# A fused attention, FFN and channel-mix kernel: first products of zeros, first values of v on GpSimd, u turned later, the last sum sorted by halves

## The chip, the core and the metric

The kernel runs on one core of a Trainium2 chip. The metric is the device time of one execution in microseconds (us). The engines are TensorE (PE in the profile, its weight loads PEld), VectorE (DVE), ScalarE (ACT), GpSimd (POOL) and SyncE (SP), which here only issues DMAs; rows named SPq and ACTq are DMAs issued by SyncE and ScalarE.

## The reference

Three layers follow each other on 4 sequences of 3072 tokens with 256 features. All is float32.

```python
scores = (1 / S) * np.matmul(z, z.transpose(0, 2, 1))     # z: 4 x 3072 x 64
attn = np.maximum(scores, 0.0) ** 2
x = u * np.matmul(attn, v)                                # u, v: 4 x 3072 x 256
h = x @ w_in                                              # 256 -> 2048
x = (h - np.tanh(h)) @ w_out                              # 2048 -> 256
x_prev = x shifted by one token within its sequence
xk = mu_k * x + (1.0 - mu_k) * x_prev
xr = mu_r * x + (1.0 - mu_r) * x_prev
k = np.maximum(xk @ w_k, 0.0)                             # 256 -> 1024
out = 1.0 / (1.0 + np.exp(-(xr @ w_r))) * (k * k @ w_v)   # 1024 -> 256
```

## The kernel before

Features lie on the partitions and tokens on the free axis. The 12288 tokens are cut into 24 tiles of 512, six to a sequence. Every float32 operand is split into a high part that TensorE's fast float32 form holds exactly and the low rest (in the code `h` and `l`), and a product is made in three passes: high by high, high by low, low by high (`PASSES`). For the scores the two parts of z lie on the two halves of the partitions, so two passes do.

The work is a list of units. For attention, unit (A, t, p) makes the scores of 256 keys by the 512 queries of tile t (4 products into a buffer `w_A`), applies relu and square on ScalarE, splits the result into h and l, and two units later (`LAG = 2`) multiplies it with v into the sum `acc_A` of its tile: 12 products, two groups of 128 keys by two halves of 128 features by three passes. Scores are symmetric: in the first tile of a sequence, units 2 to 11 also turn their block on VectorE (`keep`, tile `k`) and store it, so that later tiles load it instead of making it. After the 24 x 12 attention units come the units of the FFN (H, 8 to a tile) and of the channel mix (K, 4 to a tile, and R, one).

`produce(n)` writes unit n, `consume(n - 2)` writes the products of two units before; each engine executes its instructions in the order in which they were written. Small side work stands in a list of tasks, each with a first and a last unit between which `run_steps` puts it, within an estimated budget of VectorE time per unit. Loads are bound to a unit by `load(n, ...)`; nearly all are issued by SyncE in order.

What the change touches:

- The start (line 670 on): z groups 0 and 1 are loaded, turned on VectorE (L109), rounded (L110) and split (L87). A group of v (512 keys) is loaded as `vr`, rounded to its high part on ScalarE (L84) and its low part subtracted on VectorE (L87) in `v_steps`. Group 0 is done ahead of the first unit, groups 1 to 5 of the first sequence are tasks.
- `omu`, one minus the mixing vectors, and a `zero` column are made on VectorE at unit 1 (L693, L694).
- u of tile t is loaded in 8 pieces (`u_load`, L158), turned on VectorE (`u_turn`, L167), and multiplied with the finished sum (L487).
- The end: `out_steps` multiplies the K sum with the sigmoid (L539), turns it (L549) and stores it in 8 pieces (L554), half of the features at a time. The last tile's out_steps is the end of the kernel.

The names in the rows: `w_A` the scores, `a_A` the squared scores, `h_A` and `l_A` their parts, `acc_A` and `acc_K` the sums, `zt` and `z` the turned and the split z, `sg` the sigmoid, `o` and `ot` the result before and after its turn.

## Time and profile before

| | us |
|---|---|
| median of 3 runs (2593.69 to 2595.20) | 2593.92 |
| the profiled execution | 2593.08 |
| its span from first to last instruction | 2591.3 |
| TensorE busy, 11328 products | 2572.6 (99%) |
| VectorE busy | 1656.8 (64%) |
| ScalarE busy | 1417.3 (55%) |
| GpSimd busy, 4 instructions | 0.2 |

An engine's busy share is a mean over the whole run: VectorE's 64% is made of stretches near 100% in the first 60 us and of some 55% from the FFN on. An idle stretch matters where TensorE, which is busy 99%, waits for it. Products overlap: the duration of one (0.39 us at full pace) is longer than the distance to the next, which is what counts.

### The profile page before, as it was taken

Reading aid. Unit: us, or ns where it says so; the run is one execution under the profiler, and the core shown is the slowest. Engines: PE = TensorE matmul, PEld = TensorE weight load, DVE = VectorE, ACT = ScalarE, POOL = GpSimd, SP = SyncE. Lnnn points to the kernel's source line nnn. Section 1 sums busy time; section 2 is a strip of 40 time slices with the busy share of each in tenths; the row PEclk is TensorE's granted clock in tenths of the full one; section 3 lists DMA queues with packets and bytes.
Section 4 is the critical chain, followed back from the end, with each engine's and each line's share of the span. In section 5 each row is a group of like instructions: output and inputs, shape, how many; then the busy total and the mean of one; then the engine's idle time right before and its main releaser. Section 6 shows DMA issues by size and latency. Waiting matters only on the chain.

```text
span 2591.3 us, 28822 instructions
## 1 busy us (share of the span) xinstructions
PE 2572.6 (99%) x11328; PEld 2127.7 (82%) x11328; DVE 1656.8 (64%) x1966; ACT 1417.3 (55%) x1632; POOL 0.2 (0%) x4
## 2 busy tenths in 40 slices
PE   8999999999999999999999999999999999999998
PEld 6888888888888888888888888888888888888887
DVE  8788878887798666555555555555555555555554
ACT  7766876776587654444444444444444444444443
POOL 0000000000000000000000000000000000000000
PEclk9999999999999999999999999999999999999999
DMA  8698579668957850000000000000000000000000
GB/s 208 202 230 220 182 213 250 194 189 229 244 183 211 220 174 9 17 17 17 17 17 10 12 17 13 17 17 17 17 17 17 17 17 17 17 17 17 17 9 17
DMA packets 370680, 229.18 MB, mean 88 GB/s; under 512 B 262640, under 2 KB 336368, under 8 KB 370544
## 3 DMA queue, kind: packets, MB, share of 16 engines
q1 hardware_dynamic: 369488, 227.22, 33.3%
q8 instruction: 88, 1.44, 0.2%
q14 instruction: 48, 0.39, 0.1%
q10 hardware_dynamic: 1056, 0.13, 0.0%
HBM read 126.62 MB, written 94.63 MB: 85 GB/s over the span
## 4 chain that ended last, share of the span: by engine, by line
PE 98%; DVE 1%; ACT 0%; SPq 0%; issue 0%; DMA 0%; DVEq 0%
PE acc_A L476 29%; PE acc_H L476 20%; PE w_H L417 20%; PE acc_K L476 10%; PE w_K L417 10%; PE w_A L397 3%; PE w_A L396 3%; PE w_R L441 3%; DVE v L87 0%; SPq L99 0%; DMA vr<-in_v_dram 0%; ACT v L84 0%; ACT a_A L318 0%; SPq L158 0%; DVE k L341 0%
## 5 line engine op out<-in xcount | busy, mean ns | idle before, releaser
L476 PE MATMUL acc_H<-h_H,w_out 128*128 128x512 f32 x1536 | 504.4, 389 | 0.0
L417 PE MATMUL w_H<-xh,w_in 128*128 128x512 f32 x1536 | 500.9, 389 | 0.0
L476 PE MATMUL acc_A<-h_A,v 128*128 128x512 f32 x1344 | 441.0, 390 | 2.2 <-DVE v L87 1.8
L84 ACT ACTIVATE h_H<-g_H 128x1024 fp32r<-128x1024 f32 x192 | 203.6, 1061 | 387.0 <-DVE g_H L431 387.0
L87 DVE TENSOR_TENSOR l_H<-g_H,h_H 128x1024 fp32r<-128x1024 f32 x192 | 235.3, 1225 | 216.5 <-ACT h_H L84 216.5
L431 DVE TENSOR_TENSOR g_H<-w_H,g_H 128x1024 f32<-128x1024 f32 x192 | 233.7, 1217 | 169.4 <-ACT g_H L430 169.4
L476 PEld LDWEIGHTS acc_H<-h_H,w_out 128*128 128x128 f32 x1536 | 288.5, 188 | 59.7
L417 PEld LDWEIGHTS w_H<-xh,w_in 128*128 128x128 f32 x1536 | 288.5, 188 | 59.6
L430 ACT ACTIVATE g_H<-w_H 128x1024 f32<-128x1024 f32 x192 | 195.8, 1020 | 241.7 <-PE w_H L417 241.4
L476 PE MATMUL acc_A<-h_t,v 128*128 128x512 f32 x960 | 310.1, 389 | 0.0
L417 PE MATMUL w_H<-x,w_in 128*128 128x512 f32 x768 | 299.2, 390 | 0.0
L476 PE MATMUL acc_H<-l_H,w_out 128*128 128x512 f32 x768 | 299.1, 389 | 0.0
L476 PEld LDWEIGHTS acc_A<-h_A,v 128*128 128x128 f32 x1344 | 252.2, 188 | 56.2 <-DVE v L87 3.0
L318 ACT ACTIVATE a_A<-w_A 128x1024 f32<-128x1024 f32 (+1 forms) x169 | 172.7, 1022 | 194.1 <-PE w_A L397 193.9
L476 PE MATMUL acc_A<-l_A,v 128*128 128x512 f32 x672 | 262.2, 390 | 1.5 <-DVE l_A L87 1.0
L476 PE MATMUL acc_K<-h_K,w_v 128*128 128x512 f32 x768 | 252.1, 389 | 0.0
L417 PE MATMUL w_K<-mkh,w_k 128*128 128x512 f32 x768 | 252.0, 389 | 0.0
L87 DVE TENSOR_TENSOR l_A<-a_A,h_A 128x1024 fp32r<-128x1024 f32 (+1 forms) x169 | 201.4, 1192 | 56.5 <-ACT h_A L84 55.7
L476 PEld LDWEIGHTS acc_A<-h_t,v 128*128 128x128 f32 x960 | 180.3, 188 | 37.3
L341 DVE STREAM_TRANSPOSE k<-a_A 128x512 f32<-128x512 f32 x240 | 156.2, 689 | 83.7 <-ACT a_A L319 83.3
L322 DVE CAST h_K<-a_K 128x1024 fp32r<-128x1024 f32 x96 | 66.7, 695 | 212.8 <-ACT a_K L319 212.8
L476 PE MATMUL acc_A<-l_t,v 128*128 128x512 f32 x480 | 186.9, 389 | 0.0
(122 smaller groups left out, 3500.3 us busy)
## 6 DMA issues: line engine op xcount, KB each, us to landing
at<-k SPq DMA_DIRECT2D x120, 512.0 KB, 3.3
b<-at SPq DMA_DIRECT2D x240, 256.0 KB, 5.9
vr<-in_v_dram SPq DMA_DIRECT2D x24, 512.0 KB, 6.9
uin<-in_u_dram SPq DMA_DIRECT2D x192, 64.0 KB, 2.9
x1d<-x SPq DMA_DIRECT2D x24, 512.0 KB, 3.1
x<-x1d SPq DMA_DIRECT2D x24, 512.0 KB, 3.8
out_dram<-ot SPq DMA_DIRECT2D x192, 64.0 KB, 1.9
zin<-in_z_dram SPq DMA_DIRECT2D x94, 64.0 KB, 4.5
```

The costliest lines, as they stand in the source:

```text
L84: nc.scalar.activation(out=o, in_=i, func=ACTF.Copy)
L87: nc.vector.tensor_tensor(out=o, in0=i, in1=hi.bitcast(F32), op=ALU.subtract)
L318: nc.scalar.activation(out=a[:, x], in_=w[:, x], func=ACTF.Relu, scale=sc)
L322: high(h[:, x], a[:, x])
L341: nc.vector.transpose(out=t[:, :, :, c].rearrange("p b a j -> p a b j"), in_=a[:, c].rearrange("p (a b i) -> p a b i", a=4, b=4),)
L396: nc.tensor.matmul(w[:, j], lhsT, z1[b, g], start=True, stop=False)
L397: nc.tensor.matmul(w[:, j], lhsT, z2[t], start=False, stop=True)
L417: nc.tensor.matmul(w[:, j], ws[wt, f // 4][a][:, c, (f % 4) * P : (f % 4 + 1) * P], x[m][:, c], start=n == 0, stop=n == 3 * DC - 1,)
L430: nc.scalar.activation(out=g, in_=w, func=ACTF.Tanh)
L431: nc.vector.tensor_tensor(out=g, in0=w, in1=g, op=ALU.subtract)
L441: nc.tensor.matmul(w[:, d], ws["r", 0][a][:, c, d * P : (d + 1) * P], x[m][:, c], start=n == 0, stop=n == 3 * DC - 1,)
L476: nc.tensor.matmul(o[:, c], w[a][:, c * P : (c + 1) * P], s[m][:, j], start=p == 0 and j == 0 and n == 0, stop=p == last and j == 1 and n ...
```

## The change

Five things change.

- Ahead of the first scores, GpSimd clears a tile of zeros and TensorE makes 11 products of it into a score buffer that nobody reads.
- For the first sequence, groups 1 to 5 of v are rounded and subtracted on GpSimd instead of ScalarE and VectorE; their tasks cost nothing in the budget, their deadlines and the raw loads of groups 3 to 5 are a little earlier. Group 0 stays where it was, but is written behind the first unit instead of ahead of it. `zero` and `omu` go to GpSimd too.
- u of tile t is loaded one unit into its tile (the first at unit 5) and turned from its tile's sixth unit on; before, it was loaded a tile earlier.
- In the last K unit the 12 products are sorted by half of the features, and the last K sum lies in two buffers of one half each.
- The last tile's end works on quarters: half of the features by half of the tokens, with the four stores of each quarter alternating between SyncE's and ScalarE's queue.

```diff
--- before.py
+++ after.py
@@ -139,14 +139,21 @@
 
         def high():
             st["w"] = w = big(f"v{b}_{g}").rearrange("p (l c d) -> p l c d", l=2, c=4)
-            copy_hi(w[:, 0], vraw[b, g])
+            if b or not g:
+                copy_hi(w[:, 0], vraw[b, g])
+            else:
+                nc.gpsimd.tensor_copy(w[:, 0], vraw[b, g])
 
         def low():
             w = st["w"]
-            sub_lo(w[:, 1], vraw.pop((b, g)), w[:, 0])
+            x = vraw.pop((b, g))
+            if b or not g:
+                sub_lo(w[:, 1], x, w[:, 0])
+            else:
+                nc.gpsimd.tensor_tensor(out=w[:, 1], in0=x, in1=w[:, 0].bitcast(F32), op=ALU.subtract)
             vs[b, g] = w
 
-        return [(0.0, high), (1.3, low)]
+        return [(0.0, high), (1.3 if b else 0.0, low)]
 
     def u_load(t):
         a = p4(f"uin{t}", shape=(P, DC, 16, 32))
@@ -451,9 +458,14 @@
             split[unit] = s
 
     def get_acc(kind, t):
+        if (kind, t) not in acc and kind == "K" and t == NT - 1:
+            acc[kind, t] = [
+                ps.tile([P, 512], F32, tag="acc", name=f"acc_{kind}{t}_{c}", bufs=2) for c in range(DC)
+            ]
         if (kind, t) not in acc:
             acc[kind, t] = ps.tile([P, 2, 512], F32, tag="acc", name=f"acc_{kind}{t}", bufs=2)
-        return acc[kind, t]
+        a = acc[kind, t]
+        return a if isinstance(a, list) else [a[:, c] for c in range(DC)]
 
     def consume(unit):
         kind, t, p = unit
@@ -462,24 +474,27 @@
         s = split.pop(unit)
         o = get_acc(kind, t)
         last = {"A": NP, "H": NH, "K": NK}[kind] - 1
+        w = []
         for j in range(2):
             f = 2 * p + j
             if kind == "A":
                 kp = pairs[t % NG][p]
                 f = kp // 2 * 4 + kp % 2 + 2 * j
-            if kind == "A":
-                w = [vs[t // NG, f // 4][:, l, f % 4] for l in range(2)]
+                w.append([vs[t // NG, f // 4][:, l, f % 4] for l in range(2)])
             else:
-                w = [x[:, f % 4] for x in ws["out" if kind == "H" else "v", f // 4]]
-            for c in range(DC):
-                for n, (a, m) in enumerate(PASSES):
-                    nc.tensor.matmul(
-                        o[:, c],
-                        w[a][:, c * P : (c + 1) * P],
-                        s[m][:, j],
-                        start=p == 0 and j == 0 and n == 0,
-                        stop=p == last and j == 1 and n == 2,
-                    )
+                w.append([x[:, f % 4] for x in ws["out" if kind == "H" else "v", f // 4]])
+        order = [(j, c) for j in range(2) for c in range(DC)]
+        if unit == ("K", NT - 1, NK - 1):
+            order.sort(key=lambda x: x[1])
+        for j, c in order:
+            for n, (a, m) in enumerate(PASSES):
+                nc.tensor.matmul(
+                    o[c],
+                    w[j][a][:, c * P : (c + 1) * P],
+                    s[m][:, j],
+                    start=p == 0 and j == 0 and n == 0,
+                    stop=p == last and j == 1 and n == 2,
+                )
 
     def x1_steps(t):
         def f():
@@ -553,6 +568,24 @@
             for q in range(4):
                 nc.sync.dma_start(out=dst[q], in_=t[32 * q : 32 * q + 32, c])
 
+        def end(c, k):
+
+            o, t = st.setdefault("o", p4("o_end")), st.setdefault("t", p4("ot_end", shape=(P, DC, 16, 32)))
+            x = slice(256 * k, 256 * k + 256)
+            nc.vector.tensor_tensor(
+                out=o[:, c, x], in0=acc["K", i][c][:, x], in1=split["R", i, 0][:, c, x], op=ALU.mult
+            )
+            y = t[:, c, 8 * k : 8 * k + 8]
+            nc.vector.transpose(out=y.rearrange("p k j -> p (k j)"), in_=o[:, c, x])
+            r0 = i * TB + 256 * k
+            dst = of[r0 : r0 + 256, c * P : (c + 1) * P].rearrange(
+                "(k i) (a j) -> a i k j", i=32, j=32
+            )
+            for q in range(4):
+                (nc.sync, nc.scalar)[q % 2].dma_start(out=dst[q], in_=y[32 * q : 32 * q + 32])
+
+        if i == NT - 1:
+            return [(0.7, lambda c=c, k=k: end(c, k)) for c in range(DC) for k in range(2)]
         return [(0.7, lambda: mul(0)), (0.7, lambda: turn(0))] + [
             (0.7, lambda: mul(1)), (0.7, lambda: turn(1)),
         ]
@@ -591,13 +624,13 @@
         if g > 2:
             load(2 * g - 5, z_load, 0, g)
         if g > 1:
-            load(2 * g - 4, v_load, 0, g)
+            load(max(0, 2 * g - 5), v_load, 0, g)
         if g > 1:
             task(max(0, 2 * g - 4), 2 * g - 2, z_steps, 0, g)
-        task(max(1, 2 * g - 2), 2 * g + 1, v_steps, 0, g)
+        task(max(1, 2 * g - 2), 2 * g - 1, v_steps, 0, g)
     for t in range(NT):
-        load(t * NP - NP + 1 if t > 1 else 5 + 3 * t, u_load, t)
-        task(t * NP - 6 if t > 1 else 8 + 3 * t, t * NP + NP - 2, u_steps, t)
+        load(t * NP + (1 if t else 5), u_load, t)
+        task(t * NP + 6, t * NP + NP, u_steps, t)
         if t:
             load(t * NP - 3, z_swap, t)
         task(t * NP + NP + LAG, t * NP + NP + LAG + 3, x1_steps, t)
@@ -674,7 +707,13 @@
         v_load(0, 0)
         z_load(0, 2)
         v_load(0, 1)
-        for cost, f in z_steps(0, 0) + z_steps(0, 1) + v_steps(0, 0):
+
+        zeros = scratch("zeros").bitcast(F32R)[:, 0]
+        nc.gpsimd.memset(zeros.bitcast(F32), 0.0)
+        idle = work("idle")
+        for j in range(11):
+            nc.tensor.matmul(idle[:, j % 2], zeros[:, :P], zeros, start=True, stop=True)
+        for cost, f in z_steps(0, 0) + z_steps(0, 1):
             f()
         for m, src in ((0, moe2_mu_k), (1, moe2_mu_r)):
             with nc.allow_non_contiguous_dma(reason="a column of the mixing vector"):
@@ -689,9 +728,12 @@
             if LAG <= n < len(units) + LAG:
                 consume(units[n - LAG])
             again_high(n + 1)
+            if n == 0:
+                for cost, f in v_steps(0, 0):
+                    f()
             if n == 1:
-                nc.vector.memset(zero, 0.0)
-                nc.vector.tensor_scalar(
+                nc.gpsimd.memset(zero, 0.0)
+                nc.gpsimd.tensor_scalar(
                     out=omu, in0=mu, scalar1=-1.0, scalar2=1.0, op0=ALU.mult, op1=ALU.add
                 )
             if n >= NT * NP or is_again(n):
```

On ScalarE, the start of the program before (the squared scores of the first unit, `a_A_0`, are made in two pieces):

```order
L84 ACTIVATE z_0_174<-zt_0_169 64x512
L84 ACTIVATE v_0_182<-vr_0_160 128x1024
L318 ACTIVATE a_A_0_194<-w_A_0_189 128x512
L319 ACTIVATE a_A_0_194<-a_A_0_194 128x512
L318 ACTIVATE a_A_0_194<-w_A_0_189 128x512
L319 ACTIVATE a_A_0_194<-a_A_0_194 128x512
L318 ACTIVATE a_A_1_220<-w_A_1_215 128x1024
L319 ACTIVATE a_A_1_220<-a_A_1_220 128x1024
L84 ACTIVATE v_1_225<-vr_1_167 128x1024
```

and after the change:

```order
L84 ACTIVATE z_0_188<-zt_0_183 64x512
L325 ACTIVATE a_A_0_205<-w_A_0_200 128x512
L326 ACTIVATE a_A_0_205<-a_A_0_205 128x512
L325 ACTIVATE a_A_0_205<-w_A_0_200 128x512
L326 ACTIVATE a_A_0_205<-a_A_0_205 128x512
L84 ACTIVATE v_0_221<-vr_0_160 128x1024
L325 ACTIVATE a_A_1_236<-w_A_1_231 128x1024
L326 ACTIVATE a_A_1_236<-a_A_1_236 128x1024
L325 ACTIVATE a_A_2_253<-w_A_2_248 128x1024
```

The copy of v's group 0 has moved from ahead of the first reads of scores to behind them; that of group 1 is gone.

On VectorE, the same place before (`zt_2` and `z_0_2` are the third group of z):

```order
L87 TENSOR_TENSOR v_0_182<-vr_0_160,v_0_182 128x1024
L322 CAST h_A_0_195<-a_A_0_194 128x512
L87 TENSOR_TENSOR l_A_0_196<-a_A_0_194,h_A_0_195 128x512
L109 STREAM_TRANSPOSE zt_2_203<-zin_2_162 128x512
L110 CAST z_0_2_204<-zt_2_203 128x512
L87 TENSOR_TENSOR z_0_2_204<-zt_2_203,z_0_2_204 64x512
L322 CAST h_A_0_195<-a_A_0_194 128x512
L87 TENSOR_TENSOR l_A_0_196<-a_A_0_194,h_A_0_195 128x512
L87 TENSOR_TENSOR v_1_225<-vr_1_167,v_1_225 128x1024
L322 CAST h_A_1_221<-a_A_1_220 128x1024
L87 TENSOR_TENSOR l_A_1_222<-a_A_1_220,h_A_1_221 128x1024
```

and after the change:

```order
L329 CAST h_A_0_206<-a_A_0_205 128x512
L87 TENSOR_TENSOR l_A_0_207<-a_A_0_205,h_A_0_206 128x512
L109 STREAM_TRANSPOSE zt_2_214<-zin_2_162 128x512
L110 CAST z_0_2_215<-zt_2_214 128x512
L87 TENSOR_TENSOR z_0_2_215<-zt_2_214,z_0_2_215 64x512
L329 CAST h_A_0_206<-a_A_0_205 128x512
L87 TENSOR_TENSOR l_A_0_207<-a_A_0_205,h_A_0_206 128x512
L87 TENSOR_TENSOR v_0_221<-vr_0_160,v_0_221 128x1024
L329 CAST h_A_1_237<-a_A_1_236 128x1024
L87 TENSOR_TENSOR l_A_1_238<-a_A_1_236,h_A_1_237 128x1024
```

The subtraction for v's group 0 now stands where that of group 1 stood; the rest keeps its order.

On GpSimd, which had only four constants to write before, the start of its part of the kernel now (`ISA` is an instruction without operands that the build puts in ahead of the first subtraction):

```order
L712 MEMSET zeros 128x512
L145 CAST v_1_241<-vr_1_167 128x1024
L153 ISA
L153 TENSOR_TENSOR v_1_241<-vr_1_167,v_1_241 128x1024
L735 MEMSET head 128x1
L736 TENSOR_SCALAR head<-head 128x4
L145 CAST v_2_258<-vr_2_198 128x1024
L153 TENSOR_TENSOR v_2_258<-vr_2_198,v_2_258 128x1024
```

The pairs of groups 3 to 5 follow in the same form.

On VectorE, the end before:

```order
L322 CAST h_K_3_18984<-a_K_3_18983 128x1024
L87 TENSOR_TENSOR l_K_3_18985<-a_K_3_18983,h_K_3_18984 128x1024
L539 TENSOR_TENSOR o_19041<-acc_K_18957,sg_19015 128x512
L549 STREAM_TRANSPOSE ot_19043<-o_19041 128x512
L539 TENSOR_TENSOR o_19041<-acc_K_18957,sg_19015 128x512
L549 STREAM_TRANSPOSE ot_19043<-o_19041 128x512
```

and after the change (`acc_K_0` and `acc_K_1` are the two halves of the last sum):

```order
L329 CAST h_K_3_18999<-a_K_3_18998 128x1024
L87 TENSOR_TENSOR l_K_3_19000<-a_K_3_18998,h_K_3_18999 128x1024
L575 TENSOR_TENSOR o_end<-acc_K_0_18971,sg_19030 128x256
L579 STREAM_TRANSPOSE ot_end<-o_end 128x256
L575 TENSOR_TENSOR o_end<-acc_K_0_18971,sg_19030 128x256
L579 STREAM_TRANSPOSE ot_end<-o_end 128x256
L575 TENSOR_TENSOR o_end<-acc_K_1_18972,sg_19030 128x256
L579 STREAM_TRANSPOSE ot_end<-o_end 128x256
L575 TENSOR_TENSOR o_end<-acc_K_1_18972,sg_19030 128x256
L579 STREAM_TRANSPOSE ot_end<-o_end 128x256
```

Two steps of 512 tokens have become four of 256, and the first two read a buffer of their own.

## Rows read from the trace of the kernel before

**Rows 1.** Busy times of the page: us (share of the span) xinstructions.
```profile
PE 2572.6 (99%) x11328; PEld 2127.7 (82%) x11328; DVE 1656.8 (64%) x1966; ACT 1417.3 (55%) x1632; POOL 0.2 (0%) x4
```

**Rows 2.** The chain that ended last, in order of time: start us, us, what.
```profile
215.89 16.32 PE acc_A L476 x72
...
2577.80 5.45 PE acc_K L476 x24
```

**Rows 3.** TensorE's waits: who for whom, us in total, times, longest us.
```profile
PE w_A L396 <- DVE z L87: 6.0, 1, 6.0
PE acc_A L476 <- DVE v L87: 1.8, 3, 1.1
...
PE w_A L396 <- ACT a_A L318: 0.9, 1, 0.9
```

**Rows 4.** Timeline of the start: start us, us, engine, instruction [idle before].
```profile
6.81 0.76 PE L397 MATMUL w_A<-z,z 128*128 128x512 f32 x1
...
7.06 0.92 SPq L132 DMA_DIRECT2D vr<-in_v_dram  x1
...
8.18 1.06 ACT L84 ACTIVATE v<-vr 128x1024 fp32r<-128x1024 f32 x1 [2.75 <-DMA vr<-in_v_dram]
...
8.65 0.63 PE L397 MATMUL w_A<-z,z 128*128 128x512 f32 x1
...
9.08 0.63 PE L396 MATMUL w_A<-z 128*128 128x512 f32 x1
...
9.14 0.58 ACT L318 ACTIVATE a_A<-w_A 128x512 f32<-128x512 f32 x1
```

**Rows 5.** A stretch: start:end us, its length, busy us of PE, PEld, DVE, ACT, POOL.
```profile
11.00:40.00 29.00, 25.98 (x107) 19.76 (x108) 28.50 (x42) 23.76 (x24) 0.00 (x0) 1.00 0.75 196
```

**Rows 6.** Timeline of VectorE from 8 to 23 us, and the product behind it.
```profile
7.96 0.69 DVE L87 TENSOR_TENSOR z<-zt,z 64x512 fp32r<-64x512 f32 x1
...
10.42 0.43 DVE L322 CAST h_A<-a_A 128x512 fp32r<-128x512 f32 x1
...
10.88 0.69 DVE L87 TENSOR_TENSOR l_A<-a_A,h_A 128x512 fp32r<-128x512 f32 x1
...
14.52 1.23 DVE L87 TENSOR_TENSOR v<-vr,v 128x1024 fp32r<-128x1024 f32 x1
...
21.42 1.23 DVE L87 TENSOR_TENSOR l_A<-a_A,h_A 128x1024 fp32r<-128x1024 f32 x1
...
22.70 0.50 PE L476 MATMUL acc_A<-l_A,v 128*128 128x512 f32 x1 [0.77 <-DVE l_A L87]
```

**Rows 7.** Timeline: the first of three waits for v's low part.
```profile
38.82 0.74 PE L476 MATMUL acc_A<-h_A,v 128*128 128x512 f32 x2 [1.08 <-DVE v L87]
```

**Rows 8.** The tile vr (raw v) in the first 60 us: from issue to landing.
```profile
DMA to landing us min/median/max: 4.3/4.7/6.2
```

**Rows 9.** Timeline: one tile's u loads on SyncE, and the turn on VectorE.
```profile
96.50 5.52 SPq L158 DMA_DIRECT2D uin<-in_u_dram  x8
...
115.54 1.24 DVE L167 STREAM_TRANSPOSE uT<-uin 128x1024 f32<-128x1024 f32 x1
```

**Rows 10.** The tile uin (raw u) in the whole run: from issue to landing.
```profile
DMA to landing us min/median/max: 2.1/2.9/7.3
```

**Rows 11.** Timeline of the end: VectorE and SyncE.
```profile
2564.86 0.71 DVE L549 STREAM_TRANSPOSE ot<-o 128x512 f32<-128x512 f32 x1
...
2583.35 0.69 DVE L539 TENSOR_TENSOR o<-acc_K,sg 128x512 f32<-128x512 f32 x1 [6.84 <-PE acc_K L476]
...
2584.71 0.65 DVE L539 TENSOR_TENSOR o<-acc_K,sg 128x512 f32<-128x512 f32 x1
...
2584.81 4.18 SPq L554 DMA_DIRECT2D out_dram<-ot  x8
```

**Rows 12.** Timeline of the start: loads of z on two queues.
```profile
0.73 3.04 SPq L99 DMA_DIRECT2D zin<-in_z_dram  x6
...
0.73 0.99 ACTq L99 DMA_DIRECT2D zin<-in_z_dram  x2
```

## The prediction

> **What bounds the kernel now.** I read the page's busy shares first: TensorE is busy 99% of a span of 2591.3 us with 11328 products, VectorE 64% [rows 1]. Then the chain that ended last: in mid-run 72 products take 16.32 us, so one takes 0.2267 us, and 11328 of them 2567.7 us [rows 2]. The last 24 end at 2577.80 + 5.45 = 2583.25. Products therefore have 2583.25 - 6.0 us (the wait for the first z, [rows 3]), and need 2567.7: 9.6 us are lost between the first product and the last, 6.0 before, and 8.0 behind (2591.3 - 2583.25). The rest is products at full pace, which the change does not touch.
>
> Where the 9.6 us go, the list of TensorE's waits and the start of the timeline show. The first products come 0.43 us apart, 8.65 to 9.08, nearly twice 0.2267 (512 columns in 0.43 us are TensorE's level of 1.2 GHz, in 0.2267 us that of 2.4 GHz): seven such gaps lose some 1.4 us. Then TensorE waits 0.9 us up to 10.92, since ScalarE did not read its first results until 9.14: its read stood behind the copy of v at 8.18, which had waited 2.75 us for the load [rows 4]. What follows waits for VectorE, which is busy 28.50 of the 29 us from 11 to 40 [rows 5]; the list has three waits for v's low part, 1.8 us [rows 3]. In mid-run TensorE does not stand: the 72 products follow each other without a gap [rows 2].
>
> **The front, part one: order on ScalarE and VectorE.** z is ready as before: the change leaves the first two z turns ahead. With the clock already up, the first half of the first block is done half a microsecond after the product at 6.81, so ScalarE starts near 7.4 instead of 9.14, v's copy being behind it now. From that start to VectorE's subtraction it took 10.88 - 9.14 = 1.74 us, which gives 9.1. VectorE itself is free at 7.96 + 0.69 = 8.65 and has a 0.43 us cast first, so 9.1 again [rows 6]. The subtraction moves from 10.88 to 9.1, by 1.75 us, and so does all that follows it on VectorE up to the first l_A of a whole block, because the order shows the same eight instructions: v's first low part stands where its second stood [rows 6]. That costs something: the third product of the first sum needs this low part, which ends at 14.52 + 1.23 - 1.75 = 14.0, while before it was done ahead of the sum. TensorE has made 14 products by then. From 14.05 it makes 32 more until it needs l_A of the third block: 14.05 + 32 x 0.2267 = 21.3. That l_A ended at 21.42 + 1.23 = 22.65, and ends 1.75 us earlier (and 0.1 for the two small instructions gone to GpSimd): 20.8. So no wait there, and the product that started at 22.70 starts at 21.3: **1.4 us**.
>
> **The front, part two: five v groups leave VectorE.** VectorE loses 5 x 1.23 us, ScalarE 5 x 1.06. The three waits for v's low parts go: 1.8 us idle alone [rows 3]; each also costs a slow restart (two products take 0.74 us in the row at 38.82, where 0.2267 + 0.39 is usual) [rows 7]. From above: with TensorE's last wait at 14.05 and 14 products made, 14.05 - 6.0 - 3.2 = 4.9 us would be lost in place of 9.6, so 4.7 in all, and 3.3 for this part. I take **2.5 us**, between 1.8 and 3.3. What is late next is TensorE itself.
>
> This needs GpSimd in time. The raw group 1 is issued at 7.06 us [rows 4] and takes 4.3 to 6.2 us [rows 8], so it has landed by 13.3; its low part is wanted at 21.5, and each further one 32 products, 7.25 us, later. No row shows such a copy or subtraction on GpSimd, nor the ISA row of L153 ahead of its first subtraction. Bounds: as fast as ScalarE's copy and VectorE's subtraction, 1.06 + 1.23 = 2.3 us a pair (loss 0), or three times that, 6.9 (still inside 7.25 and 8.0, loss 0 unless the ISA row costs over 1.3 us). I take **0.3 us** lost, nearer to nothing, with 0 to 1.5 as its ends. The Trainium skill, GPSIMD Engine Reference, section Instruction dispatch, says that the first call to freshly loaded code pays an instruction load of about 6 us. No row here can show it; estimated with it, group 1 would be ready at 13.3 + 6 + 2.3 = 21.6, a tenth late, and the sum the same.
>
> **The 11 products of zeros** run while z loads: 11 x 0.43 = 4.7 us. They start behind a memset of 512 elements; no row shows one on GpSimd, so I take VectorE's cast of 512, 0.43 us [rows 6], and twice that as its ends, from some 0.7 us on: the products end between 5.8 and 6.3. The first real product is due at 6.0, the second at 6.81, so even the late end leaves 0.3 us of room: no cost. What they save is inside the 1.75 us.
>
> **u loaded and turned later** is worth nothing. Its load now stands where the next tile's stood. The tightest is tile 2: the slot of that load begins issuing at 96.50 and ends at 102.02, landing takes at most 7.3 us more, so 109.3; the turn stands where the turn at 115.54 stood [rows 9, 10]. Six microseconds of room; were it gone, VectorE would wait with the split of a block behind it.
>
> **The tail.** The last 12 products are sorted by half, so the first half is complete six products earlier, 1.36 us. VectorE starts at 2583.35 - 1.36 = 2581.99 instead. A step of multiply and turn over 512 elements takes 2584.71 - 2583.35 = 1.36 us [rows 11]; two of half the length take half of the per-element part, 0.82 each by 0.69 and 1.23 us for 512 and 1024 [rows 6]. First stores can go at 2582.85 instead of 2584.81. Before, SyncE issues 8 stores in 4.18 us, 0.52 each, and that, not VectorE, sets the end [rows 11]. Now each of two queues issues 8: 2582.85 + 4.18 = 2587.0 against 2589.0, and the landing stands behind both: **2.0 us**. Bounds: if half-sized stores issue faster, VectorE's end rules and it is 2.7; if the queues take turns, 16 x 0.52 = 8.3 us reach 2591.2 and it is 2.2 us lost. At the start SyncE issues six loads in 3.04 us while ScalarE issues two in 0.99, both at the usual half microsecond [rows 12], so I take 2.0. The first sum of the last tile now needs both buffers of acc. It begins 72 products before the end, 2583.25 - 16.32 = 2566.9, and the other buffer's last reader stands ahead of the turn at 2564.86 [rows 11]: no wait.
>
> **Sum.** -1.4 - 2.5 + 0.3 - 2.0 = -5.6 us. The profiled execution took 2593.08, 1.8 above its span; 2587.5. The median of the runs shown is 0.84 above it, so 5.6 off the median: 2588.3.
>
> **Rivals.**
> A port rival, ending slower. VectorE's subtractions read two SBUF tensors; if GpSimd's reads and these hold each other up for whole instructions, the ten GpSimd instructions sit in VectorE's fullest stretch. [...] GpSimd is idle in this trace, so no run here shows it yet. Price: at 1.5 times the 2.3 us a pair, five pairs are 17 us; turns have one input and pass, so I let a third through (an estimate), and VectorE is held up 11.5 us. Its room is the 4 x 1.23 us that part two frees, less the 2.5 counted: 2.4. TensorE is late by 9.1, and the time is 2588.3 + 9.1 = 2597.4. It decides from 8.0 us of hold-up on (2.4 + 5.6), 1.6 us a group. For: 28.50 of 29 us busy. Against: the rows only show that VectorE is full, not that GpSimd can stop it.
>
> Clock rival. Between the second and the third product of the first sum TensorE now stands 3 us (11 to 14). The 1.08 us that it stood at 38.82 left it at full pace [rows 7], which says little of 3. If the products after 14 come at 0.43 us again, eight of them lose 1.6 us: 2589.9.
>
> Late GpSimd: pairs longer than 7.25 us, or an ISA row of 9 us; 3 us of waits for v: 2591. Nothing in the rows speaks for either.
>
> Queues that take turns at the end: +2.2 in place of -2.0: 2592.5.
>
> **Chances.** Forecast 0.60, with a range of its own of 2586.5 to 2590.5; port rival 0.18; clock 0.09; late GpSimd 0.08; queues 0.05. The range that holds 8 in 10 goes from 2586.5 to 2596.5, leaving out the lucky end of the tail and the worse half of the port rival. 0.2% of the median is 5.2 us, about what can be told from no change. Below 2588.7: six tenths of the forecast and a little of the clock rival, 0.41. Above 2599.1: a fifth of the port rival, 0.04. Else 0.55.
>
> **What would show it.** Right: products 0.2267 us apart from the first real one; ScalarE's first read before 7.6; TensorE's wait list with one long wait near 14 for v's low part, and none for v after 22; VectorE's subtractions still 1.2 us; stores issued on two queues from 2582.9 less the front's gain, last at 8 issues behind. Wrong: subtractions of 2 us or gaps ahead of them while GpSimd is busy; a wait for GpSimd in TensorE's list; u turns waiting for loads; the last store over 3 us behind VectorE's end.

## The result and the profile after

The changed kernel takes 2609.10 us (median of 6 runs, 2607.27 to 2611.15) beside 2594.90 us for the kernel before (6 runs, 2593.69 to 2596.43): a ratio of 1.0055, with a 95% interval of 1.0042 to 1.0068. It is slower. The forecast was 2588.3, with a range up to 2596.5 and a chance of 0.04 for slower.

The profiled execution has a span of 2606.9 us, 15.6 more than before. To see where they went I use one measure in all that follows, the lost time: wherever a product starts more than 0.24 us behind the one before it, the excess over 0.2267 us, added up along TensorE's timeline (products of zeros left out; good to some 0.1 us). Up to 60 us it is 9.1 us before and 18.5 after; between 60 us and 1000 us it is 0.0 before and 8.5 after; behind 1000 us nothing is lost in any run. Behind the last product, 8.0 us have become 5.9 (below). 9.4 + 8.5 - 2.1 = 15.8, the difference of the spans but for 0.2.

The page's busy line of after, which answers to [rows 1]:

```profile
PE 2581.9 (99%) x11339; PEld 2132.6 (82%) x11339; DVE 1663.6 (64%) x1963; ACT 1412.9 (54%) x1627; POOL 21.5 (1%) x17
```

TensorE has the same products and 11 more, but 9.3 us more busy time: the 11 products of zeros take 4.25 us, and products that follow each other at half pace count for longer. VectorE has lost five subtractions (5 x 1.23 = 6.2 us) and is busier by 6.8. That already says that something slows VectorE's instructions themselves.

TensorE's waits in after (who for whom, us in total, times, longest us), beside [rows 3]:

```profile
PE acc_A L491 <- DVE v L87: 5.2, 1, 5.2
PE acc_A L491 <- DVE h_A L329: 3.5, 1, 3.5
PE acc_A L491 <- DVE l_A L87: 3.2, 5, 0.9
PE acc_A L491 <- DVE l_t L87: 2.2, 1, 2.2
PE acc_A L491 <- ACT h_A L84: 1.8, 1, 1.8
PE idle L715 <- POOL zeros L712: 1.3, 1, 1.3
PE w_A L403 <- ACT a_A L325: 0.9, 1, 0.9
```

The 6.0 us for the first z are gone from the list only because the products of zeros run there: the first real product starts at 5.87 (6.0 before). The 1.3 us ahead of those products cost nothing. No wait names GpSimd's v parts, so GpSimd is in time. All other new waits are for VectorE or ScalarE: 5.2 us for the low part of v's group 0, 3.5 for a cast, and three in mid-run (for `l_A`, one of its five; for `l_t`; and for `h_A` on ScalarE).

VectorE's timeline from 11.9 us on (start us, us):

```profile
11.92 1.15 DVE L329 CAST h_A<-a_A 128x512 fp32r<-128x512 f32 x1
13.11 2.72 DVE L87 TENSOR_TENSOR l_A<-a_A,h_A 128x512 fp32r<-128x512 f32 x1
15.75 1.21 DVE L87 TENSOR_TENSOR v<-vr,v 128x1024 fp32r<-128x1024 f32 x1
16.88 1.52 DVE L329 CAST h_A<-a_A 128x1024 fp32r<-128x1024 f32 x1
18.44 3.28 DVE L87 TENSOR_TENSOR l_A<-a_A,h_A 128x1024 fp32r<-128x1024 f32 x1
...
22.93 2.77 DVE L87 TENSOR_TENSOR z<-zt,z 64x512 fp32r<-64x512 f32 x1
25.72 1.30 DVE L348 STREAM_TRANSPOSE k<-a_A 128x512 f32<-128x512 f32 x2
26.95 2.64 DVE L329 CAST h_A<-a_A 128x1024 fp32r<-128x1024 f32 x1
29.62 1.23 DVE L87 TENSOR_TENSOR l_A<-a_A,h_A 128x1024 fp32r<-128x1024 f32 x1
```

and GpSimd's beside it:

```profile
11.76 1.04 POOL L145 CAST v<-vr 128x1024 fp32r<-128x1024 f32 x1 [10.50 <-DMA vr<-in_v_dram]
12.88 2.40 POOL L153 TENSOR_TENSOR v<-vr,v 128x1024 fp32r<-128x1024 f32 x1
...
15.82 2.04 POOL L145 CAST v<-vr 128x1024 fp32r<-128x1024 f32 x1
17.94 2.69 POOL L153 TENSOR_TENSOR v<-vr,v 128x1024 fp32r<-128x1024 f32 x1
```

Subtractions of 512 elements that took 0.69 us [rows 6] take 2.72 and 2.77, one of 1024 takes 3.28 in place of 1.23. The first ends at 15.83, 0.55 us behind GpSimd's subtraction beside it (12.88 + 2.40 = 15.28), that of 1024 at 21.72, 1.09 us behind GpSimd's (20.63): about what each takes by itself, as if it had not begun before. Casts are late too (1.15 for 0.43, 1.52 and 2.64 for 0.65). Turns are not: 1.30 for two, as ever. With GpSimd done, at 29.62, a subtraction takes 1.23 again. All excesses of this kind up to 45 us add to 12.7 us, 8.2 on subtractions and 4.5 on casts.

What the first wait does to TensorE (its timeline; a row with x2 is two products):

```profile
17.01 1.22 PE L491 MATMUL acc_A<-h_A,v 128*128 128x512 f32 x2 [5.23 <-DVE v L87]
18.03 0.63 PE L491 MATMUL acc_A<-l_A,v 128*128 128x512 f32 x1
18.46 1.05 PE L491 MATMUL acc_A<-h_A,v 128*128 128x512 f32 x2
...
29.73 0.76 PE L491 MATMUL acc_A<-h_A,v 128*128 128x512 f32 x1 [3.51 <-DVE h_A L329]
```

Behind the 5.23 us without a product the products come 0.43 us apart, at the level of 1.2 GHz, up to 21.45; behind the 3.51 us again, up to 35.27. The stretch from 11 to 40 us, which [rows 5] shows at a granted clock of 1.00, is at 0.76 in after:

```profile
11.00:40.00 29.00, 19.81 (x64) 15.07 (x65) 27.30 (x26) 12.31 (x12) 17.08 (x11) 0.76 0.58 147
```

VectorE is busy 27.30 of the 29 us with 26 instructions, where it did 42 before.

At the end (VectorE, then the two queues; [rows 11]):

```profile
2599.76 0.42 DVE L575 TENSOR_TENSOR o_end<-acc_K,sg 128x256 f32<-128x256 f32 x1 [5.48 <-PE acc_K L491]
...
2602.58 0.45 DVE L579 STREAM_TRANSPOSE ot_end<-o_end 128x256 f32<-128x256 f32 x1
...
2600.69 3.86 SPq L585 DMA_DIRECT2D out_dram<-ot_end  x8
...
2600.69 3.92 ACTq L585 DMA_DIRECT2D out_dram<-ot_end  x8
```

The last product ends at 2601.01, the span 5.9 us behind it, 8.0 before: 2.1 us gained. The two queues issue at the same time, eight stores each. At the start, ScalarE reads its first scores earlier, as the forecast had it (9.14 in [rows 4]):

```profile
7.64 0.60 ACT L325 ACTIVATE a_A<-w_A 128x512 f32<-128x512 f32 x1 [2.35 <-PE w_A L404]
```

### The profile page after: what moved, and what is told of

The parts are those of the page before. It is cut to its first block, busy times and chain, and to the rows that moved or that the text cites. A ratio compares the mean times of both kernels' runs of the same rounds, so it can differ in the third digit from the quotient of the medians.

```text
span 2606.9 us, 28885 instructions
## 1 busy us (share of the span) xinstructions
PE 2581.9 (99%) x11339; PEld 2132.6 (82%) x11339; DVE 1663.6 (64%) x1963; ACT 1412.9 (54%) x1627; POOL 21.5 (1%) x17
## 4 chain that ended last, share of the span: by engine, by line
PE 95%; DMA 2%; DVE 1%; SPq 1%; ACT 1%; issue 1%; DVEq 0%; ACTq 0%
PE acc_A L491 27%; PE w_H L424 20%; PE acc_H L491 20%; PE w_K L424 10%; PE acc_K L491 10%; PE w_A L404 3%; PE w_A L403 3%; PE w_R L448 3%; DMA b<-at 1%; DMA wr_in<-wd_in 0%; SPq L165 0%; DMA uin<-in_u_dram 0%; SPq L365 0%; DMA c_k<-in_moe_w_k_dram 0%; DVE h_A L329 0%
## 5 line engine op out<-in xcount | busy, mean ns | idle before, releaser
L87 DVE TENSOR_TENSOR l_A<-a_A,h_A 128x1024 fp32r<-128x1024 f32 (+1 forms) x169 | 207.8, 1230 | 62.5 <-ACT h_A L84 61.7
```

Source lines behind the costliest of these rows:

```text
L87: nc.vector.tensor_tensor(out=o, in0=i, in1=hi.bitcast(F32), op=ALU.subtract)
```

## The experiments

Two theories, one for each part of the loss. **P**: GpSimd's v groups hold up VectorE (front). **U**: the move of u makes the three mid-run waits. The rivals were late v parts, TensorE's clock by itself, and for U the question of which half of the move does it, the loads or the turns. Every table row has the lost time up to 60 us, from there to 1000 us, the span of the profiled run and the median. The runs were made on several chips, and each ratio is to the runs of the kernel before on the same chip (medians of 2594.76 to 2596.73).

| run | to 60 | 60 to 1000 | span | median | ratio to before (95%) |
|---|---|---|---|---|---|
| before | 9.1 | 0.0 | 2591.3 | 2594.90 | |
| after | 18.5 | 8.5 | 2606.9 | 2609.10 | 1.0055 (1.0042 to 1.0068) |
| undo_v | 9.3 | 10.6 | 2600.2 | 2603.76 | 1.0033 (1.0020 to 1.0045) |
| undo_u | 18.2 | 0.5 | 2598.8 | 2600.80 | 1.0024 (1.0014 to 1.0034) |
| undo_uv | 8.8 | 0.3 | 2589.1 | 2592.06 | 0.9990 (0.9981 to 0.9999) |
| tail_only | 9.1 | 2.7 | 2591.9 | 2591.72 | 0.9989 (0.9980 to 0.9998) |
| u_load_early | 17.4 | 4.0 | 2601.6 | 2603.69 | 1.0034 (1.0021 to 1.0046) |
| u_blank | 18.1 | 8.8 | 2606.9 | 2608.13 | 1.0046 (1.0033 to 1.0058) |
| gp_reads | 19.1 | 0.9 | 2600.1 | 2602.03 (one run) | |
| gp_writes | 11.3 | 2.3 | 2593.6 | 2595.59 (one run) | |
| v_free | 6.8 | 0.0 | 2586.9 | 2589.91 | 0.9983 (0.9974 to 0.9992) |
| fill | 16.4 | 1.1 | 2597.5 | 2599.49 | 1.0018 (1.0009 to 1.0027) |
| best | 7.8 | 1.2 | 2588.9 | 2590.87 | 0.9984 (0.9975 to 0.9993) |
| best_fill | 7.1 | 1.3 | 2588.5 | 2590.01 | 0.9976 (0.9967 to 0.9985) |

**undo_v**: v's groups 1 to 5 back on ScalarE and VectorE, with their old dates; the rest as changed.

```diff
-            if b or not g:
-                copy_hi(w[:, 0], vraw[b, g])
-            else:
-                nc.gpsimd.tensor_copy(w[:, 0], vraw[b, g])
+            copy_hi(w[:, 0], vraw[b, g])
...
-            load(max(0, 2 * g - 5), v_load, 0, g)
+            load(2 * g - 4, v_load, 0, g)
...
-        task(max(1, 2 * g - 2), 2 * g - 1, v_steps, 0, g)
+        task(max(1, 2 * g - 2), 2 * g + 1, v_steps, 0, g)
```

> The changed kernel with v's groups 1 to 5 of the first sequence on ScalarE and VectorE again (their loads, deadlines and budget as before); zeros, u, end and the two small instructions on GpSimd as changed. Theory P (GpSimd's reads hold VectorE's two-input subtractions and casts up): every VectorE subtraction of 1024 elements in the first 60 us takes 1.2 us again and none 2.6 to 3.3; what TensorE loses in the first 60 us falls from 18.6 us to 8 to 9, so the span falls by about 10 us to 2597; products stay at full pace from 5.9 us on. Theory C (the clock and the order of v's group 0 cost the time, GpSimd being harmless): the wait for v's low part near 14 stays at 5 us and half pace after it, and the span stays above 2604. The mid-run waits near 669, 710 and 957 us (8.5 us) stay under both.

**undo_u**: u loaded and turned as before; the rest as changed.

```diff
-        load(t * NP + (1 if t else 5), u_load, t)
-        task(t * NP + 6, t * NP + NP, u_steps, t)
+        load(t * NP - NP + 1 if t > 1 else 5 + 3 * t, u_load, t)
+        task(t * NP - 6 if t > 1 else 8 + 3 * t, t * NP + NP - 2, u_steps, t)
```

> The changed kernel with u loaded and turned as before; v on GpSimd, zeros and end as changed. Theory U (u's 8 loads, one tile later in SyncE's order, push blocks and weights that TensorE waits for): the mid-run waits near 669, 710 and 957 us go, 8.5 us, the span falls to about 2598.5; the first 60 us stay at 18 to 19 us lost. Rival (the later start of everything after a slower front shifts loads against each other): mid-run waits of some 8 us stay or move, span above 2604.

**undo_uv**: both edits.

> Both undone: what is left of the change are the products of zeros, v's group 0 behind the first unit, the two small instructions on GpSimd and the end in quarters. If P and U add up: span 2591.3 - 0.6 (start) - 2.2 (end) = 2588.5, time near 2592. If they share a cause, one of undo_v or undo_u alone already reaches this, and this one brings nothing more.

**tail_only**: the kernel before with the new end alone (`end`, the two acc buffers, the sorted products).

> The kernel before with the new end alone (last K unit sorted by half, quarters, stores on two queues). All theories: from the last product's end to the span's end 5.9 us in place of 8.0, the rest as before: span 2589.1, time about 2.1 us under that of before. If two queues took turns it would be 2 us over.

The two parts separate cleanly. Without GpSimd's groups the front is at 9.3 in place of 18.5, without the move of u mid-run is at 0.5 in place of 8.5; with both undone the kernel is 2.9 us below before (2594.94 in the runs of that chip), and the new end alone gives 3.2, so the end is all that the change gains, as far as these runs can tell.

Two expectations were missed. In undo_v the products behind the wait of 2.48 us at 14.42 come at half pace, not at full pace, and its span is 3 us over the one expected: the mid-run losses are larger than in after (10.6 for 8.5), though nothing of u differs. Most of that lies near 948.5 us, where TensorE stood 2.25 us and went on at half pace; in after it stood 1.78 us there and went on at full pace. That a TensorE which has lost less before comes earlier and so waits longer fits this, but was not tested by itself. In tail_only the profiled run lost 2.7 us between 240 and 247 us (last section), so its span, not its median, is 2.8 us over the one expected.

**gp_reads** and **gp_writes** tell a hold-up by GpSimd's work from v parts that are late: undo_uv with work on GpSimd that nobody waits for.

```diff
+                gsp = big("spare").bitcast(F32)[:, :1024]
+                nc.gpsimd.tensor_copy(gsp[:, :512], vraw[0, 0][:, :2].rearrange("p c d -> p (c d)"))
+                nc.gpsimd.memset(gsp[:, 512:], 0.0)
+                for i in range(5):
+                    nc.gpsimd.tensor_copy(gsp, gsp)
+                    nc.gpsimd.tensor_tensor(out=gsp, in0=gsp, in1=gsp, op=ALU.subtract)
```

In gp_writes the loop is `for i in range(17): nc.gpsimd.memset(gsp, 0.0)`.

> The kernel with v and u as before and the new end, and on GpSimd, from the landing of the first v group on, five casts and five subtractions of 128x1024 in a tile that nothing else uses, some 18 us of work that nobody waits for. Theory, the reads: GpSimd reading SBUF holds up VectorE's casts and subtractions. Then VectorE's subtractions of 128x1024 beside it take over 2.5 us where 1.2 is usual and the casts of 128x512 over 1 us where 0.43 is usual, turns stay at 0.65 each, and TensorE loses about 18 us up to 60 us, 9 more than the 9.2 without the extra work: span near 2598. Rival: the change was slow because v's parts came late from GpSimd; then extra work that nobody waits for costs nothing, and the span is near 2589.

> As the kernel with the extra work on GpSimd, but the ten instructions that read SBUF are 17 memsets of 128x1024, which only write, for about the same 18 us. Theory, the reads: VectorE's casts and subtractions keep 0.43, 0.65 and 1.2 us, TensorE loses 9 to 9.5 us up to 60 us, span near 2589. Rival, any work of GpSimd's on SBUF: casts and subtractions are held up as beside the reads, about 18 us lost, span near 2598.

VectorE's timeline in gp_reads:

```profile
9.97 1.40 DVE L88 TENSOR_TENSOR l_A<-a_A,h_A 128x512 fp32r<-128x512 f32 x1
...
13.45 1.41 DVE L88 TENSOR_TENSOR z<-zt,z 64x512 fp32r<-64x512 f32 x1
14.88 2.00 DVE L323 CAST h_A<-a_A 128x512 fp32r<-128x512 f32 x1
...
18.25 4.88 DVE L88 TENSOR_TENSOR v<-vr,v 128x1024 fp32r<-128x1024 f32 x2
```

and in gp_writes, where 17 memsets run from 9.67 to 28.47:

```profile
9.67 18.80 POOL L730 MEMSET spare<- 128x1024 f32 x17
```

```profile
12.12 0.69 DVE L88 TENSOR_TENSOR z<-zt,z 64x512 fp32r<-64x512 f32 x1
...
13.91 2.35 DVE L88 TENSOR_TENSOR v<-vr,v 128x1024 fp32r<-128x1024 f32 x2
...
18.78 1.27 DVE L111 CAST z<-zt 128x512 fp32r<-128x512 f32 x1
...
22.01 1.51 DVE L323 CAST h_A<-a_A 128x1024 fp32r<-128x1024 f32 x1
```

P is shown: work of which nobody needs the result costs the front 10 us, about as much as the v groups did (18.2 in undo_u for 8.8 in undo_uv). A subtraction is held up by GpSimd's reading instructions alone; beside memsets it takes 0.69 and 2.35 / 2 = 1.18 us, as if GpSimd were idle. A cast can be held up by either, 1.27 for 0.43 and 1.51 for 0.65 beside memsets (three of the five casts beside the 17 memsets; two took 0.43 and 0.69); neither theory had said that, and it makes TensorE's wait for group 0 3.22 us in gp_writes for 2.48 in undo_uv, with products at half pace behind it; hence 11.3 and 8.8. The subtractions of 1024 took 2.44 each, not "over 2.5".

**v_free** asks for the forecast's front without its price: groups 1 to 5 of the first sequence are loaded but not split, their products take group 0's parts (so the first sequence's output is another one); u as before.

```diff
+            if not b and g:
+                return
...
+            if not b and g:
+                vs[b, g] = vs[0, 0]
+                return
```

> The changed kernel with u as before, and groups 1 to 5 of the first sequence's v not split at all: their products take the parts of group 0, so the output of the first sequence is not the reference's; all loads, products and the rest stay. It is the forecast's front without its price on GpSimd. Theory: VectorE relieved of five subtractions, with GpSimd idle, loses nothing after the wait for group 0's low part: 5.3 us lost up to 60 us (4.1 less than the 9.4 of before, as the forecast had it: 1.4 + 2.5 and the 0.3 of GpSimd's lateness not paid), span near 2591.3 - 4.1 - 2.2 = 2585.0, median near 2588. Rival: VectorE is still the bound with its other work, or ScalarE is: 7 us or more lost up to 60 us, median of 2590 or more.

6.8 us, between the two. The only long wait for VectorE is the 2.48 us ahead of the third product of the first sum, which the forecast had; but the products behind it come at half pace up to 17.99. Without that stretch it is 5.3.

```profile
14.71 1.22 PE L490 MATMUL acc_A<-h_A,v 128*128 128x512 f32 x2 [2.48 <-DVE v L87]
15.73 0.63 PE L490 MATMUL acc_A<-l_A,v 128*128 128x512 f32 x1
```

**fill** prices the half pace in the changed front: undo_u with products of zeros in the two long waits, 20 in the first and 14 in the second (`nil` is a tile of zeros).

```diff
...
+        if unit == ("A", 0, 2):
+            fill(o[0], 14)
...
+                if unit == ("A", 0, 0) and j == c == 0 and n == 2:
+                    fill(o[0], 20)
```

> The changed kernel with u as before, and products of zeros in the two long waits of the front: 20 behind the second product of the first sum, 14 ahead of the sum of the third block. They add zero to the sum, so the output is the reference's. Theory, both causes: GpSimd's hold-up of VectorE makes the waits, and each wait puts TensorE at half pace for some nine products behind it (0.43 us apart, 2.0 us lost each time). With the waits filled the pace stays at 0.2267; the first 2 us come back as a longer wait for VectorE at 29.7, the second are kept as far as VectorE had been waiting for TensorE (1.37 us at 38.8): 16.8 lost up to 60 us in place of 18.2, span near 2597.4, median near 2599.4. Rival, the clock is the main price: 4 us come back, 14.2 lost, median near 2596.8. Rival, the pace costs nothing since VectorE is late by itself: 18.2 lost, median near 2600.8.

The pace behind both is 0.2267, and 1.8 us of 18.2 come back, 1.3 us in the median: "both causes", nearly to the number. The half pace is a consequence of the waits and worth a tenth of the 18.2 us.

**u_load_early**: the changed kernel with u's loads at their old units and its turns late. **u_blank**: the changed kernel with a blank step of 1.1 in the planner's count (the estimated VectorE time by which `run_steps` puts side steps between the units) at the turn's old place and the moved turn counting nothing, so that VectorE has all other instructions in the old order. In the rows of this part `uin` is raw u, `c_k` a raw piece of the weights w_k, `wr_in` the weights w_in before their split, `b` a turned block of squared scores loaded again, `h_t` and `l_t` its parts.

```diff
-        load(t * NP + (1 if t else 5), u_load, t)
+        load(t * NP - NP + 1 if t > 1 else 5 + 3 * t, u_load, t)
```

```diff
-        return [(1.1, lambda: u_turn(t))]
+        return [(0.0, lambda: u_turn(t))]
...
+        blank = lambda t: [(1.1, lambda: None)]
+        task(t * NP - 6 if t > 1 else 8 + 3 * t, t * NP + NP - 2, blank, t)
```

> The changed kernel with u's loads back in their old places; u's turns stay late, and GpSimd keeps the five v groups. Theory, the loads: what made TensorE wait at 669.8, 710.4 and 956.8 us (8.15 us of lost time) is that each u load's eight transfers stand on SyncE's queue ahead of the loads of b, c_k and wr_in that the splits wait for. Then those losses go: less than 1.5 us lost behind 60 us, span near 2599, median near 2601, as with u wholly as before. Rival, the turns: a turn of 1.2 us on VectorE in the middle of a tile is what makes the splits late; then the 8 us stay and the median is near 2609.

> The changed kernel (u loaded and turned late, v on GpSimd); only the planner's count is changed: a blank step of 1.1 stands where u's turn stood before, and the turn itself counts nothing at its new place. So VectorE has every instruction but u's turns in the order of the kernel with u as before. Theory, the order: taking the turn out of its old place let the steps of c and z run one block earlier, ahead of their loads, and VectorE, with the split of a block behind it, waits for c_k (3.9 us at 663) and zin (5.9 us at 702); those waits and what TensorE loses at 669.8 and 710.4 (1.19 + 3.88) go, while the 3.08 at 956.8, where the last tile's u load now stands ahead of the weights' loads, stay: 2.5 to 3.5 us lost behind 60 us, median near 2604. Rival, the loads: all 8.15 us stay, median near 2609. Rival, the late turn's own 1.2 us on VectorE: the losses move but stay near 8 us.

My theory of the loads was half wrong. With the loads back, the loss at 956.8 is gone, but 2.31 us at 669.8 and 1.69 at 718 to 724 stay. With the order back, it is the other way round: nothing at 669.8 and 710, and 6.8 us at 954 (most of the other 2 us of u_blank are waits like those of the last section). So two mechanisms. The first, in after, on VectorE:

```profile
667.08 0.43 DVE L211 TENSOR_SCALAR cw_k<-c_k 128x512 int32<-128x512 int32 x1 [3.86 <-DMA c_k<-in_moe_w_k_dram]
...
668.49 1.22 DVE L87 TENSOR_TENSOR l_A<-a_A,h_A 128x1024 fp32r<-128x1024 f32 x1
...
707.69 0.71 DVE L109 STREAM_TRANSPOSE zt<-zin 128x512 f32<-128x512 f32 x1 [5.90 <-DMA zin<-in_z_dram]
```

and in undo_u the same two instructions of VectorE, in the old order:

```profile
667.34 1.22 DVE L87 TENSOR_TENSOR l_A<-a_A,h_A 128x1024 fp32r<-128x1024 f32 x1 [2.10 <-ACT h_A L84]
...
672.03 0.42 DVE L211 TENSOR_SCALAR cw_k<-c_k 128x512 int32<-128x512 int32 x1
```

SyncE in after:

```profile
650.18 7.72 SPq L165 DMA_DIRECT2D uin<-in_u_dram  x8
...
659.96 0.45 SPq L190 DMA_DIRECT2D c_k<-in_moe_w_k_dram  x1
```

u's loads stand at the same place on SyncE before and after (650.28 in undo_u), since a shift by a whole tile puts one tile's loads where the next one's were. What moved is the turn: without its 1.1 in the planner's count the first step on c_k comes a block earlier, before its load has landed, VectorE waits, and `l_A`, which has no need of c_k, stands behind it. At 707.69 a z turn does the same ahead of the low parts `l_t`, the loss at 710.4; in u_blank VectorE waits for neither load there (1.01 us for zin at 711). The second mechanism, in u_blank (SyncE, ScalarE, TensorE):

```profile
923.10 6.97 SPq L165 DMA_DIRECT2D uin<-in_u_dram  x8
...
937.36 0.82 SPq L256 DMA_DIRECT2D wr_in<-wd_in  x1
...
949.16 1.06 ACT L84 ACTIVATE w_in<-wr_in 128x1024 fp32r<-128x1024 f32 x1 [5.76 <-DMA wr_in<-wd_in]
...
954.30 0.79 PE L491 MATMUL acc_A<-h_A,v 128*128 128x512 f32 x1 [3.02 <-ACT h_A L84]
```

The last tile has no next one: its eight loads are new in that place, 7 us of SyncE ahead of the weights, and ScalarE, with the split of a block behind its copy of `w_in`, waits for them. The expectation of 2.5 to 3.5 us there failed in size: 6.8, because TensorE came 3.7 us earlier than in after and the weights only 2.5 (949.16 for 951.65); it stood 3.02 us instead of 1.78 and went on at half pace. So taking one of the two waits away hardly pays: 2608.13 for 2609.10.

**best**: undo_uv with v's groups 3 to 5 loaded as early as in the change and split two blocks earlier. **best_fill**: that, ten products of zeros in the wait of 2.5 us, and the turn of z's group 3 and v's groups 1 and 2 a block later.

```diff
-            load(2 * g - 4, v_load, 0, g)
+            load(max(0, 2 * g - 5), v_load, 0, g)
...
-        task(max(1, 2 * g - 2), 2 * g + 1, v_steps, 0, g)
+        task(max(1, 2 * g - (3 if g > 2 else 2)), 2 * g - 1, v_steps, 0, g)
```

> The kernel with v and u as before and the new order at the start and the new end, with one difference: v's groups 3 to 5 are loaded as early as in the change, and their casts and subtractions stand two blocks earlier on ScalarE and VectorE, ahead of other work there. Theory: the waits for v's low part at 38.5 and for the low parts at 46.4 and 54.3 (1.38 + 0.62 + 0.62 us lost) come from v's casts standing late on ScalarE, and go: 6.2 to 7 us lost up to 60 us, span near 2586.6, median near 2589.5. Rival: VectorE is full up to 38 us, and the work put ahead makes other subtractions late instead: 9 us lost as before, median near 2592.

> The kernel with v and u as before, v's groups 3 to 5 early, and two things more: ten products of zeros in the wait of 2.5 us ahead of the third product of the first sum (they add zero), and the third z turn and v's groups 1 and 2 each a block later on VectorE, behind the low parts that TensorE wants first. Theory, the clock: that wait alone puts TensorE at half pace for some seven products in the runs before (0.43 us apart from 14.5 to 17.9); filled, 1.5 us come back there, less what VectorE, full up to 37 us, cannot follow: 5.3 to 6.2 us lost up to 60 us in place of 7.8, span near 2587, median near 2589.5. Rival: VectorE is the bound and takes it all back: 7.5 us or more lost up to 60 us, median near 2591. Rival: the half pace comes from something else than the wait (the first load, the start): products behind the filled wait are 0.43 us apart all the same.

In best the waits for v at 38.5, 46.4 and 54.3 are gone, but the stretch at half pace behind 14.46 is there, 1.5 us, which undo_uv had not behind the same wait; so 7.8, not 6.2 to 7. In best_fill the products behind the filled wait come at full pace:

```profile
11.68 2.47 PE L487 MATMUL acc_A<-z,nil 128*128 128x512 f32 x10
14.34 0.73 PE L488 MATMUL acc_A<-h_A,v 128*128 128x512 f32 x2 [0.19 <-DVE v L88]
14.90 0.39 PE L488 MATMUL acc_A<-l_A,v 128*128 128x512 f32 x1
...
25.76 0.50 PE L488 MATMUL acc_A<-l_A,v 128*128 128x512 f32 x1 [0.47 <-DVE l_A L88]
```

5.1 us are lost at 15 us, but VectorE takes 2 us back later, by two waits for l_A and the restarts behind them (0.74 and 1.14): 7.1 lost, not the 5.3 to 6.2 expected. It is the fastest kernel here that computes the whole output, 2590.01, below before and after; its intervals and those of best, undo_uv and tail_only overlap, so which of the four is best is not shown.

## Why the prediction was wrong, step by step

- **Part two, GpSimd in time, VectorE relieved** is the step that failed. GpSimd was in time (pairs of 3.5 to 4.8 us, inside the 7.25), as the step argued, but that was the wrong question: its sum left VectorE's other instructions at their old durations and put nothing for what GpSimd does to them. The port rival, at 0.18, is what happened, by its mechanism: 12.7 us of hold-up for the 11.5 estimated; less the room of 2.4, plus 1.8 for the half pace (fill), that gives 12.1 of the 12.5 us by which the front missed its 6.0. Measured by itself, the work on GpSimd costs 11.4 us (18.2 in undo_u for 6.8 in v_free), where the rival had 9.1. That its 11.5 came so near is in part luck: it let casts through, and they are held up as well, 4.5 of the 12.7 us.
  The Trainium skill, SBUF — State Buffer, section Who interferes with whom, has both rules: subtractions with two SBUF inputs against GpSimd's reads, and casts, which can run in a mode that takes two ports, against any of its work. The rival's price has the first and let casts pass with all else that has one input; gp_reads and gp_writes agree with the page in each (0.69 kept beside memsets, 1.41 beside reads; up to 1.27 for 0.43 in a cast beside memsets).
  I gave the rival 0.18 because "the rows only show that VectorE is full". That was the sign to weigh the other way: with 28.50 of 29 us busy [rows 5], nearly every hold-up reaches TensorE.
- **Part one, the order** came nearly as described: ScalarE's first read at 7.64 (forecast 7.4), VectorE's first `l_A` at 9.39 (9.1), the long wait moved to the third product of the first sum. By itself, with v on VectorE, it is worth 0.3 us (8.8 for 9.1), since there the subtractions of groups 0 and 1 stand one behind the other (from 13.16 in undo_uv) and the third block's `l_A` ends only 0.3 us earlier; with VectorE relieved without GpSimd (v_free) the front is 2.3 us better, against 1.4 + 2.5 in the sum. The missing 1.6 is the **clock rival**, at its size: the half pace behind that wait of 2.5 us, which v_free, best and undo_v show and undo_uv does not.
- **u "worth nothing"** failed too, 8.5 us. The step measured room at tile 2, a load against its own turn. That room was there; no u turn waits. What it left out was who changes place with the moved instructions: the planner's other steps, which went ahead of their loads, and the weights behind the last tile's u on SyncE. The order of the program showed both.
- **GpSimd's lateness** and the ISA row: no loss. The cast ends at 12.80 and the subtraction behind the ISA row starts at 12.88. The Trainium skill, GPSIMD Engine Reference, section Instruction dispatch, gives about 6 us for first calls of newly loaded code; this trace does not show it.
- **The 11 products of zeros**: right, no cost; the memset took 0.53 us for the 0.43 assumed. That the products behind the first real one come at full pace: right (6.67 to 8.13).
- **The tail**: 2.1 us for 2.0. Right; the queues do not take turns. **No wait for two acc buffers**: right.

In the sum: the front 18.5 in place of 6.0, mid-run 8.5 in place of nothing, the tail 0.1 better: 20.9 of the 21.2 us between the forecast span (2585.7) and the measured one.

## What to carry to other kernels

An idle engine is not free room when its instructions hold up those of the one that is full: ask what its instructions do to the neighbour's while both run, and let that decide before asking whether it is in time. When a step is moved, look at what takes its old place as much as at its new one, on the engine and on the queue, and at the first and last tile, where nothing is shifted in behind it. A wait that is removed alone can give nothing when a second late thing stands behind it.

## What the runs showed that I had not expected

- VectorE's casts (one input) can be held up by GpSimd's memsets: three of the five beside the 17 memsets of gp_writes took 0.80 to 1.51 us for 0.43 and 0.65. Its subtractions are held up by GpSimd's reads only, its turns by nothing that ran there.
- GpSimd is held up in return: its cast of 128x1024 takes 1.04 to 1.11 us by itself and 2.04 beside VectorE's subtractions.
- A wait of 2.48 us in TensorE is followed by full pace in undo_uv and by half pace in v_free, best and undo_v, with the same products around it. In the runs here the pace was full behind every wait of 1.1 us and half behind every one of 3 us and more; between 2.0 and 2.5 us both occur (2.04 at 669.8 in u_load_early: full; 2.19 at 710.4 in after: half). What decides is open.
- Near 240 to 250 us a wait for the exchange of z's halves (`z<-z`) or for l_A costs up to 2.7 us in some profiled runs and nothing in others (before, v_free, u_load_early); in u_blank there is another near 488 us. With one profile of each kernel, whether it belongs to the kernel or to the execution is open. It makes most of the 2.8 us between the profiled spans of undo_uv and tail_only, whose medians are alike.
